# Loading the first weight chunk beside the first input tile, copies by PSUM bank and no GpSimd loads, in a two-layer feed-forward kernel

## Chip, cores, metric

One core of one Trainium2 chip. The metric is the device time of the core in microseconds (us), lower is better. A "run" is one execution; medians are over runs. "Head" is what happens from the start of the program until TensorE begins its steady stream of products.

## The reference, cut

```python
B, S, D, F = 1, 2048, 576, 4608          # all bfloat16
def reference(x, w1, b1, w2, b2):
    h = einsum("bsd,df->bsf", x, w1) + b1
    r = where(h > 0, h, 0)
    return einsum("bsf,fd->bsd", r * r, w2) + b2
```

## The kernel before

The rows of x are handled in four blocks of 512. For the first product x must lie transposed in SBUF (`xT`). For blocks 1 to 3 a DMA transposes it; block 0 is transposed by TensorE, 128 x 128 at a time. D = 576 is four chunks of 128 and one of 64. The first four column tiles of w1 (512 columns, `w1n`, chunks k = 0..3; `w1n8` is the 64-row rest) are loaded first and used while the remainder of w1 (`w1_h`, in column pieces and two 64-row halves) is coming.

The warm-up products and the first eight loads:

```python
wps = ps_o.tile([P, 512], FP32, name="wps", tag="po")
WARM = [512] * 6 + [128]
for i, n in enumerate(WARM):
    keep(nc.tensor.matmul(wps[:, 0:n], lhsT=ones[:, 0:P], rhs=ones[:, 0:n], start=True, stop=True))
# ...
load_x(nc.sync, 0)
load_x(nc.scalar, 1)
load_w1n(nc.sync, 0)
load_x(nc.scalar, 2)
load_w1n(nc.sync, 1)
load_x(nc.sync, 3)
for k in range(2, NK):
    load_w1n(nc.sync, k)
# ...
nc.gpsimd.dma_start(out=b1_rows[0:NFT, :], in_=b1.rearrange("(ft p) -> ft p", p=P))
nc.gpsimd.dma_start(out=b2_col[:], in_=b2[DM:D].rearrange("(d o) -> d o", o=1))
```

The head on TensorE. `x_transpose(j, k)` transposes chunk k of x tile j; `part(h, k)` is four products of 256 columns for half h of the block:

```python
for j in range(2):
    for k in range(NK):
        x_transpose(j, k)
for j in range(2):
    x_transpose(j, NK)
x_copies(0)            # PSUM to SBUF: chunks 0 to 3 have a bank each; VectorE and ScalarE by turns
part(0, 0)
for k in range(NK + 1):
    x_transpose(2, k)
part(0, 1)
part(0, 2)
for k in range(NK + 1):
    x_transpose(3, k)
x_copies(1)
dup_windows(0)
part(0, 3)
part(1, 0)
make_b1T()
for k in range(1, NK):
    part(1, k)
```

Then come pairs of 64-row products (`pair`, at the end of block 0's first four column tiles), and `a_rows`, which uses w1_h column by column: 18 products a column. Each load on a hardware queue waits, by the compiled program's semaphores, for the landing of the load eight places ahead of it, so at most eight are under way (in the changed kernel the ninth load is issued at 3.48 us, when the first of ScalarE's queue has landed at 3.47).

## Time and profile before

| | before |
|---|---|
| time, first three runs | 290.86 us median (290.51 to 291.31) |
| span of the profiled run | 289.6 us |
| x tile 0 landed; first transpose | 3.73; 3.77 us |
| first product of `part` | 4.87 us |
| TensorE at full clock from (clock record of the trace) | 6.51 us |
| first 64-row pair | 9.85 us |
| from there to the last product's end | 277.03 us |

The page of the kernel before: the span, busy time by engine, and the chain that ended last (each line there is an engine, a tile and a line of the kernel, with its share of the span).

```profile
span 289.6 us, 4693 instructions
...
PE 285.5 (99%) x2027; PEld 139.9 (48%) x2032; DVE 78.6 (27%) x176; ACT 96.7 (33%) x154; POOL 2.3 (1%) x10
...
PE 98%; DMA 1%; issue 0%; DVE 0%
```

TensorE is the bound, all the way. The only place with another limit is the head. The start of the chain of waits of before (start, duration, what; "x10" counts merged instructions; a piece begins where the one before it ends):

```profile
0.73 2.99 DMA x_sb<-in_x_dram
3.73 0.04 issue
3.77 1.25 PE tb L149 x10
5.02 0.86 PE pn L227 x4
5.88 0.53 PE tb L149 x5
6.42 0.98 PE pn L227 x8
7.40 0.28 PE tb L149 x5
7.68 0.87 PE pn L227 x8
```

Read the pace: four products in 0.86 us (215 ns each), later eight in 0.87 (109 ns each); five transposes in 0.53 us, later in 0.28. TensorE runs at half clock until about 6.5 us, and from 3.77 us on the chain is TensorE alone. No load after x tile 0 is on it.

### The profile page before, as it was taken

To read this page: it belongs to the slowest core of one execution; us is meant where nothing else is said; L and a number is where in the kernel's file an instruction comes from. 1 tells how busy PE (TensorE), PEld (TensorE's weight loads), DVE (VectorE), ACT (ScalarE), POOL (GpSimd) and SP (SyncE) were. 2 spreads that over 40 slices of the span, in tenths; PEclk is the share of its full clock that TensorE was granted. 3 is DMA by queue.
4 is the path that set the end of the run, shared out by engine and by line. 5 is a ranking of instruction groups with operands and counts; after the bars stand their busy time and mean duration, and the time that the engine had idled before them with its cause. 6 is when DMAs were issued, how large, how long until landed. Compare 5 with 4: busy or idle time off the path is not lost.

```text
span 289.6 us, 4693 instructions
## 1 busy us (share of the span) xinstructions
PE 285.5 (99%) x2027; PEld 139.9 (48%) x2032; DVE 78.6 (27%) x176; ACT 96.7 (33%) x154; POOL 2.3 (1%) x10
## 2 busy tenths in 40 slices
PE   8999999999999999999999999999999999999996
PEld 5544444444444555555544444444444455555555
DVE  1644554444500200000015444444440001100001
ACT  2566666666500000000027666666670000000000
POOL 3000000000000000000000000000000000000000
PEclk9999999999999999999999999999999999999999
DMA  7999999400001200000000000000000110000000
GB/s 198 221 245 188 308 389 212 92 0 2 0 14 25 52 16 18 16 16 18 16 16 2 1 2 0 2 0 2 0 2 0 36 38 16 16 16 19 33 16 18
DMA packets 31605, 16.52 MB, mean 57 GB/s; under 512 B 15700, under 2 KB 31584, under 8 KB 31584
## 3 DMA queue, kind: packets, MB, share of 16 engines
q1 hardware_dynamic: 31232, 15.91, 22.3%
q10 hardware_dynamic: 288, 0.30, 0.4%
q8 instruction: 16, 0.26, 0.4%
q14 instruction: 5, 0.04, 0.0%
q0 software_dynamic: 64, 0.01, 0.0%
HBM read 11.36 MB, written 2.36 MB: 47 GB/s over the span
## 4 chain that ended last, share of the span: by engine, by line
PE 98%; DMA 1%; issue 0%; DVE 0%
PE ph L188 42%; PE po L289 38%; PE pt L270 11%; PE pn L209 4%; PE pn L227 1%; DMA x_sb<-in_x_dram 1%; PE tb L149 1%; PE ph L190 1%; PE pn L203 1%; DVE o_sb L291 0%; PE b1T_ps L166 0%; PE pn L205 0%
## 5 line engine op out<-in xcount | busy, mean ns | idle before, releaser
L190 PE MATMUL ph<-xTw,w_h 64*128 64x512 bf16 x576 | 124.6, 376 | 0.0
L188 PE MATMUL ph<-xTw,w_h 64*128 64x512 bf16 x576 | 124.6, 376 | 0.0
L289 PE MATMUL po<-w_sb,hT 128*128 128x448 bf16 (+2 forms) x612 | 109.4, 341 | 0.0
L176 ACT ACTIVATE r<-ph,b1T 128x512 bf16<-128x512 f32 x128 | 81.1, 685 | 41.6 <-PE ph L190 41.6
L188 PEld LDWEIGHTS <-w_h 64*128 64x128 bf16 x576 | 54.1, 94 | 68.3
L289 PEld LDWEIGHTS <-hT 128*128 128x128 bf16 x612 | 58.5, 98 | 51.0
L177 DVE TENSOR_TENSOR hT<-r 128x512 bf16<-128x512 bf16 x144 | 61.2, 426 | 75.9 <-ACT r L176 75.5
L190 PEld LDWEIGHTS <-w_h 64*128 64x128 bf16 x576 | 54.1, 94 | 0.0
L291 DVE TENSOR_TENSOR o_sb<-po,b_bc 128x448 bf16<-128x448 f32 (+2 forms) x17 | 10.2, 597 | 125.8 <-PE po L289 125.8
L270 PE MATMUL pt<-hT,w_sb 128*128 128x512 bf16 x142 | 31.3, 379 | 0.1
L176 ACT ACTIVATE r<-pn,b1T 128x512 bf16<-128x512 f32 x16 | 10.3, 688 | 61.0 <-PE pn L205 59.6
L270 PEld LDWEIGHTS <-w_sb 128*128 128x128 bf16 x144 | 14.1, 98 | 17.0
L273 ACT ACTIVATE oT<-pt,b2T 128x512 bf16<-128x512 f32 x4 | 2.8, 688 | 28.3 <-PE pt L270 28.3
L209 PE MATMUL pn<-xTw,w1n 128*128 128x512 bf16 x45 | 10.4, 379 | 0.4 <-issue 0.3
L209 PEld LDWEIGHTS <-w1n 128*128 128x128 bf16 x48 | 4.5, 98 | 6.0 <-issue 0.8
L227 PE MATMUL pn<-xTw,w1n 128*128 128x256 bf16 x32 | 4.6, 295 | 0.0
L63 PE MATMUL wps<-const-bfloat16-1.0 128*128 128x512 bf16 (+1 forms) x7 | 2.8, 582 | 0.8 <-PEq L344 0.8
L227 PEld LDWEIGHTS <-w1n 128*128 128x128 bf16 x32 | 3.3, 107 | 0.5
L156 DVE COPY xTw<-tb 128x256 bf16<-128x256 bf16 x4 | 1.1, 292 | 6.7 <-PE tb L149 6.7
L119 DVE COPY xTw<-xTw 64x2048 bf16<-64x2048 bf16 x4 | 2.8, 690 | 0.2
L120 DVE COPY xTw<-xTw 64x2048 bf16<-64x2048 bf16 x4 | 2.7, 687 | 0.1
L149 PE MATMUL tb<-ident,x_sb 128*128 128x128 bf16 x20 | 2.4, 288 | 0.2 <-DMA x_sb<-in_x_dram 0.2
(23 smaller groups left out, 15.2 us busy)
## 6 DMA issues: line engine op xcount, KB each, us to landing
w_sb<-in_w_dram SPq DMA_DIRECT2D x4, 1296.0 KB, 12.7
w_h<-in_w_dram SPq DMA_DIRECT2D x14, 288.0 KB, 6.2
out_dram<-o_sb SPq DMA_DIRECT2D x15, 112.0 KB, 1.7
w_h<-in_w_dram SPq DMA_DIRECT2D x4, 144.0 KB, 3.5
w1n<-in_w_dram SPq DMA_DIRECT2D x4, 128.0 KB, 3.9
out_dram<-ot SPq DMA_DIRECT2D x4, 128.0 KB, 2.0
x_sb<-in_x_dram ACTq DMA_DIRECT2D x2, 144.0 KB, 2.9
x_sb<-in_x_dram SPq DMA_DIRECT2D x2, 144.0 KB, 3.4
```

The costliest lines, as they stand in the source:

```text
L63: keep(nc.tensor.matmul(wps[:, 0:n], lhsT=ones[:, 0:P], rhs=ones[:, 0:n], start=True, stop=True))
L149: keep(nc.tensor.transpose(bank[:, slot, qc], xs[:, j, c0:c0 + P], ident[:]))
L176: keep(nc.scalar.activation(out=r[:], in_=bank[:], func=ACT.Relu, bias=b1T[:, ft:ft + 1], scale=1.0))
L177: keep(nc.vector.tensor_tensor(out=hTs[sb][:, ft, :], in0=r[:], in1=r[:], op=ALU.mult))
L188: keep(nc.tensor.matmul(bx[:], lhsT=w1_h[0:H, LO_C[i], jc], rhs=xT[0:H, LO_W[i], :], start=(i == 0), stop=(i == NC - 1)))
L190: keep(nc.tensor.matmul(by[:], lhsT=w1_h[H:P, UP_C[i], jc], rhs=xT[H:P, UP_W[i], :], start=(i == 0), stop=(i == NC - 1)))
L203: keep(nc.tensor.matmul(banks[2 * i][:], lhsT=w1n8[0:H, i, :], rhs=xT[0:H, SPC, :], start=start, stop=stop, skip_group_check=order == "k_o ...
L209: keep(nc.tensor.matmul(banks[g][:], lhsT=w1n[:, k, g * P:(g + 1) * P], rhs=xT[:, O + k, :], start=start, stop=stop))
L227: keep(nc.tensor.matmul(banks[g][:, hc], lhsT=w1n[:, k, g * P:(g + 1) * P], rhs=xT[:, O + k, hc], start=(h == 0 and k == 0), stop=False, s ...
L270: keep(nc.tensor.matmul(pt[:], lhsT=w2_sb[:, ft, DM:D], rhs=hT[:, ft, :], start=(i == 0), stop=(i == NFT - 1)))
L289: keep(nc.tensor.matmul(po[:, 0:d1 - d0], lhsT=hT[:, ft, jj * P:(jj + 1) * P], rhs=w2_sb[:, ft, d0:d1], start=(i == 0), stop=(i == NFT - 1)))
L291: keep(nc.vector.tensor_tensor(out=o_sb[:, d0:d1], in0=po[:, 0:d1 - d0], in1=b2_bc[:, d0:d1], op=ALU.add))
```

## The change

The intent: have w1 chunk 0 as early as x tile 0, so that the first products can start; spread the other loads evenly over two queues; take the two small bias loads away from GpSimd; put several transposed chunks in one PSUM bank and copy bank by bank; fill the idle time ahead of x tile 0 by a longer last warm-up product (the warm-up products are called the filler below).

```diff
-    WARM = [512] * 6 + [128]
+    WARM = [512] * 6 + [256]
...
     load_x(nc.sync, 0)
-    load_x(nc.scalar, 1)
-    load_w1n(nc.sync, 0)
+    load_w1n(nc.scalar, 0, 1)
+    load_x(nc.sync, 1)
     load_x(nc.scalar, 2)
-    load_w1n(nc.sync, 1)
-    load_x(nc.sync, 3)
-    for k in range(2, NK):
-        load_w1n(nc.sync, k)
+    load_w1n(nc.sync, 1, 2)
+    load_x(nc.scalar, 3)
+    load_w1n(nc.sync, 2, 3)
+    load_w1n(nc.scalar, 3, 4)
...
-    nc.gpsimd.dma_start(out=b1_rows[0:NFT, :], ...)
-    nc.gpsimd.dma_start(out=b2_col[:], ...)
     keep(nc.scalar.activation(out=warm[:], ...))
+    keep(nc.scalar.dma_start(out=b1_rows[0:NFT, :], ...))   # b2_col: later, by SyncE
+    for h in range(2):
+        load_w1n8(nc.sync, h)          # all 512 columns to both halves; now ahead of w1_h
...
-    tb_po = [ps_o.tile([P, 2, HS], BF16, name="tb", tag="po") for _ in range(2)]
-    tb_ph = [ps_h.tile([P, 2, HS], BF16, name="tb", tag="ph") for _ in range(4)]
+    tb = [[ps_h.tile([P, 4, HS], BF16, name="tb", tag="ph") for _ in range(2)] for _ in range(2)]
+    PLACE = [(0, 0), (0, 1), (1, 0), (1, 1), (1, 2)]
...
+    def x_transpose(j):                # all five chunks of one tile; copies after the second tile
+        h, q = divmod(j, 2)
+        for bank, ks in enumerate((T_ORDER[:2], T_ORDER[2:])):
+            for k in ks:
+                ...transpose into tb[h][bank]
+            for k in ks if q == 1 else ():
+                copy = nc.scalar.copy if h == 1 and k in (2, 3) else nc.vector.tensor_copy
+                keep(copy(out=xT0[:, w, hc], in_=tb[h][bank][:, PLACE[k][1], :]))
...
                 for j in range(2):
-                    for k in range(NK):
-                        x_transpose(j, k)
...
+                    x_transpose(j)
+                for k in range(2):
+                    part(0, k)
+                    x_transpose(2 + k)
                 dup_windows(0)
+                for k in range(2, NK):
+                    part(0, k)
```

Also w2 is loaded in two pieces instead of four, and block 0's accumulators all lie in one pool.

More of the change, by code (lines that the diff above doesn't have):

```diff
@@ L57 @@
     ps_o = ctx.enter_context(tc.tile_pool(name="ps_o", bufs=4, space=PSUM))
-    wps = ps_o.tile([P, 512], FP32, name="wps", tag="po")
+    wps = ps_h.tile([P, 512], FP32, name="wps", tag="ph")
     ones = nc.const_aps.tensor(1.0, [P, 512], BF16)
-    WARM = [512] * 6 + [128]
+    WARM = [512] * 6 + [256]
     for i, n in enumerate(WARM):
@@ L66 @@
     w1n = wpool.tile([P, NK, GW], BF16, name="w1n")
-    w1n8 = wpool.tile([P, G // 2, P], BF16, name="w1n8")
+    w1n8 = wpool.tile([P, GW], BF16, name="w1n8")
     w1_h = wpool.tile([P, NC, FH], BF16, name="w1_h")
@@ L72, in load_x, with load_w1n @@
         keep(eng.dma_start(out=xs[:, rt, :], in_=x2[rt * P:(rt + 1) * P, :]))
-    def load_w1n(eng, k):
-        keep(eng.dma_start(out=w1n[:, k, :], in_=w1[k * P:(k + 1) * P, 0:GW]))
+    def load_w1n(eng, k0, k1):
+        src = w1[k0 * P:k1 * P, 0:GW].rearrange("(k p) f -> p k f", p=P)
+        keep(eng.dma_start(out=w1n[:, k0:k1, :], in_=src))
     def load_w1n8(eng, h):
-        src = w1[NK * P:D, 0:GW].rearrange("p (i h f) -> p i h f", h=2, f=P)
-        keep(eng.dma_start(out=w1n8[h * H:(h + 1) * H, :, :], in_=src[:, :, h, :]))
+        keep(eng.dma_start(out=w1n8[h * H:(h + 1) * H, :], in_=w1[NK * P:D, 0:GW]))
     def load_w1(eng, h, j0, j1):
@@ L83, in load_w1 @@
                       in_=w1_v[:, :, GW + h * FH + j0 * P:GW + h * FH + j1 * P]))
+    b1_rows = const.tile([P, P], BF16, name="b1_rows")
+    nc.vector.memset(b1_rows[:], 0.0)
     load_x(nc.sync, 0)
-    load_x(nc.scalar, 1)
-    load_w1n(nc.sync, 0)
+    load_w1n(nc.scalar, 0, 1)
+    load_x(nc.sync, 1)
     load_x(nc.scalar, 2)
-    load_w1n(nc.sync, 1)
-    load_x(nc.sync, 3)
-    for k in range(2, NK):
-        load_w1n(nc.sync, k)
+    load_w1n(nc.sync, 1, 2)
+    load_x(nc.scalar, 3)
+    load_w1n(nc.sync, 2, 3)
+    load_w1n(nc.scalar, 3, 4)
     ident = const.tile([P, P], BF16, name="ident")
     make_identity(nc, ident[:])
-    b1_rows = const.tile([P, P], BF16, name="b1_rows")
-    nc.gpsimd.memset(b1_rows[:], 0.0)
-    nc.gpsimd.dma_start(out=b1_rows[0:NFT, :], in_=b1.rearrange("(ft p) -> ft p", p=P))
-    b2_col = const.tile([P, 1], BF16, name="b2_col")
-    nc.gpsimd.dma_start(out=b2_col[:], in_=b2[DM:D].rearrange("(d o) -> d o", o=1))
-    b2T = const.tile([P, 1], FP32, name="b2T")
-    nc.gpsimd.tensor_copy(out=b2T[:], in_=b2_col[:])
     warm = const.tile([P, 1], FP32, name="warm")
     keep(nc.scalar.activation(out=warm[:], in_=nc.const_aps.tensor(0.0, [P, 1], FP32), func=ACT.Relu))
+    keep(nc.scalar.dma_start(out=b1_rows[0:NFT, :], in_=b1.rearrange("(ft p) -> ft p", p=P)))
+    for h in range(2):
+        load_w1n8(nc.sync, h)
     E3, O, SPC, E = 0, 1, 5, 6
@@ L130 @@
     w2_view = w2.rearrange("(ft p) d -> p ft d", p=P)
-    W2CH = 9
+    W2CH = 18
     def load_w2(c):
@@ L140 @@
     HS = SB // 2
-    tb_po = [ps_o.tile([P, 2, HS], BF16, name="tb", tag="po") for _ in range(2)]
-    tb_ph = [ps_h.tile([P, 2, HS], BF16, name="tb", tag="ph") for _ in range(4)]
-    half_banks = [tb_ph, None]
-    def x_transpose(j, k):
+    tb = [[ps_h.tile([P, 4, HS], BF16, name="tb", tag="ph") for _ in range(2)] for _ in range(2)]
+    PLACE = [(0, 0), (0, 1), (1, 0), (1, 1), (1, 2)]
+    T_ORDER = [0, 1, 2, 3, NK]
+    def x_transpose(j):
         h, q = divmod(j, 2)
-        qc = slice(q * P, (q + 1) * P)
-        bank, slot, c0 = (half_banks[h][k], 0, k * P) if k < NK else (half_banks[h][2], 1, D - P)
-        keep(nc.tensor.transpose(bank[:, slot, qc], xs[:, j, c0:c0 + P], ident[:]))
-    def x_copies(h):
         hc = slice(h * HS, (h + 1) * HS)
-        for k in range(NK):
-            src = half_banks[h][k][:, 0, :]
-            if k % 2 == 0:
-                keep(nc.vector.tensor_copy(out=xT0[:, O + k, hc], in_=src))
-            else:
-                keep(nc.scalar.copy(out=xT0[:, O + k, hc], in_=src))
-        keep(nc.vector.tensor_copy(out=xT0[:, E3, hc], in_=half_banks[h][2][:, 1, :]))
+        for bank, ks in enumerate((T_ORDER[:2], T_ORDER[2:])):
+            for k in ks:
+                slot = PLACE[k][1]
+                c0 = k * P if k < NK else D - P
+                keep(nc.tensor.transpose(tb[h][bank][:, slot, q * P:(q + 1) * P], xs[:, j, c0:c0 + P], ident[:]))
+            for k in ks if q == 1 else ():
+                w = O + k if k < NK else E3
+                copy = nc.scalar.copy if h == 1 and k in (2, 3) else nc.vector.tensor_copy
+                keep(copy(out=xT0[:, w, hc], in_=tb[h][bank][:, PLACE[k][1], :]))
     b1T = const.tile([P, NFT], FP32, name="b1T")
     def make_b1T():
-        b1T_ps = ps_o.tile([P, P], BF16, name="b1T_ps", tag="po")
+        b1T_ps = ps_h.tile([P, P], BF16, name="b1T_ps", tag="ph")
         keep(nc.tensor.transpose(b1T_ps[:], b1_rows[:], ident[:]))
@@ L198, in a_full @@
         for g in range(G):
-            pool, tag = (ps_o, "po") if g < 2 else (ps_h, "ph")
+            pool, tag = (ps_o, "po") if g < 2 or order == "k_outer" else (ps_h, "ph")
             banks.append(pool.tile([P, SB], FP32, name="pn", tag=tag))
         def pair(i, start, stop):
-            keep(nc.tensor.matmul(banks[2 * i][:], lhsT=w1n8[0:H, i, :], rhs=xT[0:H, SPC, :],
+            keep(nc.tensor.matmul(banks[2 * i][:], lhsT=w1n8[0:H, 2 * i * P:(2 * i + 1) * P], rhs=xT[0:H, SPC, :],
                              start=start, stop=stop, skip_group_check=order == "k_outer"))
-            keep(nc.tensor.matmul(banks[2 * i + 1][:], lhsT=w1n8[H:P, i, :], rhs=xT[H:P, E3, :],
+            keep(nc.tensor.matmul(banks[2 * i + 1][:], lhsT=w1n8[H:P, (2 * i + 1) * P:(2 * i + 2) * P], rhs=xT[H:P, E3, :],
                              start=start, stop=stop, skip_group_check=order == "k_outer"))
@@ L220, in a_full @@
             if order == "k_outer":
-                tb_new = [ps_h.tile([P, 2, HS], BF16, name="tb", tag="ph") for _ in range(2)]
-                half_banks[1] = tb_new + tb_po
                 def part(h, k):
@@ L231, in a_full @@
                 for j in range(2):
-                    for k in range(NK):
-                        x_transpose(j, k)
-                for j in range(2):
-                    x_transpose(j, NK)
-                x_copies(0)
-                part(0, 0)
-                for k in range(NK + 1):
-                    x_transpose(2, k)
-                part(0, 1)
-                part(0, 2)
-                for k in range(NK + 1):
-                    x_transpose(3, k)
-                x_copies(1)
+                    x_transpose(j)
+                for k in range(2):
+                    part(0, k)
+                    x_transpose(2 + k)
                 dup_windows(0)
-                part(0, 3)
+                for k in range(2, NK):
+                    part(0, k)
                 part(1, 0)
@@ L296 @@
         load_w1(nc.sync, 1, j0, j1)
-        if j0 == 0:
-            load_w1n8(nc.sync, 0)
-            load_w1n8(nc.sync, 1)
     load_xT(1)
@@ L303 @@
         load_w1(nc.sync, 1, j0, j1)
+    b2_col = const.tile([P, 1], BF16, name="b2_col")
+    keep(nc.sync.dma_start(out=b2_col[:], in_=b2[DM:D].rearrange("(d o) -> d o", o=1)))
+    b2T = const.tile([P, 1], FP32, name="b2T")
+    nc.gpsimd.tensor_copy(out=b2T[:], in_=b2_col[:])
     keep(nc.sync.dma_start(out=b2_bc[:], in_=b2.partition_broadcast(P)))
-    for c in (0, 2, 1, 3):
+    for c in range(2):
         load_w2(c)
```

## The prediction

> **What bounds the kernel.** The page's first part has TensorE busy 285.5 of 289.6 us; the chain of waits is 98% TensorE. From the first L203 pair (9.85 us) to the last product (286.9 us) the matmul timeline has no gap over 0.16 us, and is left alone. Only the head can move.
>
> **The head of before** (matmul timeline, single instructions):
> - Seven warm-up matmuls from 0.78; then 0.17 us idle until x tile 0 lands at 3.73.
> - From 3.77 TensorE has practically no idle: 20 transposes, the b1 transpose, 32 products of 256 columns. No load is late: w1 chunks landed at 4.32, 5.86, 6.47, 7.05, used at 4.87, 6.21, 6.69, 7.51.
> - The clock record reaches full speed only at 6.51. Before it a transpose takes 107 ns and a 256-column product 213 ns; after it 56 and 109. At full speed all 53 need 21 x 0.056 + 32 x 0.109 = 4.7 us; 2.74 us at half clock cost 1.37 us more: 3.77 + 4.7 + 1.37 = 9.8, as seen.
>
> The Trainium skill ("TensorE: Matmul & The Clock Gate", Part 1) says the array runs at half rate until a busy window of a free-running 3.4 us counter has passed, so the moment varies between runs. The trace agrees: full speed 5.74 us after the first matmul.
>
> **What the change does.**
> - x0 still goes first on SyncE beside one load of like size: landing at 3.6 to 3.75. x1 becomes second on SyncE (issued at 1.2; the load in that place landed at 4.32). It is needed after five x0 transposes, at 3.77 + 5 x 0.107 = 4.30: just in time, perhaps 0.1 us late.
> - First copy: VectorE copies take 0.29 us. The first product starts at about 4.95 instead of 4.87.
> - No GpSimd loads: those packets ran from 3.65 to 5.3 us, while the DMA rate fell from 350 to 170-215 GB/s. Without them later loads should land 0.5 to 1 us earlier, but TensorE didn't wait for them.
> - The b1 load moves behind the ACT table load (1.28 us): issued at about 4.3, landed at about 7, needed at 8.3.
> - w1n8 grows by 64 KB and moves ahead of w1_h. w1_h columns 2 to 4 landed at 13.16, used at about 14.2: still in time.
> - Banks, w2 in two loads, b2 by SyncE: off the path. 128 more warm-up columns (0.107 us) fill idle time.
>
> On the critical path: -0.1 (x0, filler) + 0.1 (x1, first copy) - 0.1 (smaller waits, clock) = about -0.1 us. The clock's phase is larger: a switch 1 us earlier or later should (estimate) move the end by 0.5 us, which fits the spread of before, 290.51 to 291.31.
>
> **Predicted: 290.7 us, 8 in 10 between 290.1 and 291.3.** Faster by over 2%: 1%; within 2%: 98%; slower by over 2%: 1%.
>
> **What would show it.** Right: x0 lands within 0.2 us of 3.7; first 256-column product at 4.8 to 5.0; first 64-row pair at 9.2 to 10.2, following the start of full clock by half; no DMA dip at 4.2 to 5.2 us; 277 us from the first pair to the last product. Wrong: idle TensorE before the x1 or b1 transposes; a wait for w1_h at its second or third column.
>
> **What would make it wrong.** Full clock coming systematically earlier: up to 1 us faster. x1 or b1 late: up to 0.5 us slower.

## More of the kernel before

One trap. The windows view has a column for the granted clock, the last but two (the columns are the window, its length, busy time of PE, PEld, DVE, ACT and POOL, clock, DMA share, GB/s). For the kernel before:

```profile
0.80:3.60 2.80, 2.80 (x7) 0.84 (x7) 0.00 (x0) 1.49 (x2) 1.80 (x5) 1.00 0.63 184
4.20:5.10 0.90, 0.90 (x10) 0.82 (x9) 0.33 (x2) 0.47 (x2) 0.00 (x0) 1.00 0.87 197
```

It says 1.00 where the products run at half pace, because the first clock record comes only at the switch to full speed. In a head, trust the pace of equal products, not this column.

## The result, and the profile after

| | before | after |
|---|---|---|
| time, six runs each | 290.92 us (290.51 to 291.52) | 291.15 us (290.95 to 291.52) |
| span of the profiled run | 289.6 | 289.2 |
| x0 landed; first transpose | 3.73; 3.77 | 3.66; 3.70 |
| first product of `part` | 4.87 | 5.11 |
| full clock from | 6.51 | 4.51 |
| first 64-row pair | 9.85 | 9.49 |
| from there to the last product's end | 277.03 | 277.03 |

The ratio of the changed kernel to before is 1.0008 with a 95% interval of 0.9994 to 1.0022: the same within noise. A ratio is the mean time of one kernel's fast runs over that of the other's fast runs of the same rounds, so it is not quite the ratio of the medians quoted.

The page of the changed kernel, the same lines:

```profile
span 289.2 us, 4697 instructions
...
PE 285.5 (99%) x2032; PEld 139.1 (48%) x2032; DVE 79.0 (27%) x179; ACT 96.1 (33%) x152; POOL 0.9 (0%) x7
...
PE 99%; DVE 0%; issue 0%
```

And the chain of waits of its head:

```profile
0.77 2.93 PE wps L63 x7
3.71 0.71 PE tb L150 x5
4.42 0.00 issue
4.42 0.33 PE tb L150 x2
4.74 0.02 issue
4.77 0.30 DVE xTw L154
5.07 0.04 issue
5.11 0.60 PE pn L218 x4
5.71 0.28 PE tb L150 x5
5.99 0.44 PE pn L218 x4
6.42 0.28 PE tb L150 x5
```

Full clock came 2 us earlier here than in the profile of before (four products take 0.44 us at 5.99), which by itself should take 1 us from the head. The head was only 0.36 us shorter. The difference went into waits that before did not have: the transposes of x1 start at 4.42, though those of x0 were done issuing at 3.70 + 5 x 0.107 = 4.24; and a VectorE copy stands on the chain, for which TensorE waits from 4.74 to 5.11.

So the first question was whether the change had brought the early clock. The second was where the rest went.

### The profile page after: what moved, and what is told of

It is laid out like the page before. It is cut to its first block, busy times and chain, and to the rows that moved or that the text cites. A ratio compares the mean times of both kernels' runs of the same rounds, so it can differ in the third digit from the quotient of the medians.

```text
span 289.2 us, 4697 instructions
## 1 busy us (share of the span) xinstructions
PE 285.5 (99%) x2032; PEld 139.1 (48%) x2032; DVE 79.0 (27%) x179; ACT 96.1 (33%) x152; POOL 0.9 (0%) x7
## 4 chain that ended last, share of the span: by engine, by line
PE 99%; DVE 0%; issue 0%
PE ph L182 42%; PE po L272 38%; PE pt L253 11%; PE pn L203 4%; PE pn L218 1%; PE wps L63 1%; PE ph L184 1%; PE pn L197 1%; PE tb L150 1%; DVE xTw L154 0%; DVE o_sb L274 0%; PE b1T_ps L160 0%; PE pn L199 0%
## 5 line engine op out<-in xcount | busy, mean ns | idle before, releaser
L218 PE MATMUL pn<-xTw,w1n 128*128 128x256 bf16 x32 | 4.0, 273 | 0.2 <-DVE xTw L154 0.2
L154 DVE COPY xTw<-tb 128x256 bf16<-128x256 bf16 x8 | 1.9, 284 | 4.9 <-PE tb L150 4.6
L197 PE MATMUL pn<-xTw,w1n 64*128 64x512 bf16 x8 | 2.4, 379 | 0.0
```

The lines of the kernel that those rows point to most:

```text
L197: keep(nc.tensor.matmul(banks[2 * i][:], lhsT=w1n8[0:H, 2 * i * P:(2 * i + 1) * P], rhs=xT[0:H, SPC, :], start=start, stop=stop, skip_grou ...
L218: keep(nc.tensor.matmul(banks[g][:, hc], lhsT=w1n[:, k, g * P:(g + 1) * P], rhs=xT[:, O + k, hc], start=(h == 0 and k == 0), stop=False, s ...
```

## The experiments

**The sum used below.** All 21 transposes and 32 products of the head take about 4.7 us at full clock (21 x 0.056 + 32 x 0.109). So

*first 64-row pair = first transpose + 4.7 + half of the time from there to full clock + waits.*

For before: 3.77 + 4.7 + 1.37 = 9.84 against 9.85 measured, waits 0. For after: 3.70 + 4.7 + 0.40 = 8.80 against 9.49, waits 0.69 us.

Two theories. A: the moment of full clock is chance; a late clock hides late loads, an early one lays them bare, and the change made the loads and copies that matter later. B: the change itself (its longer filler) brought the early clock.

### Both kernels again: e1, e2, e10

No edit; each gives a second or third profile, and five runs.

> The kernel before, unchanged, for a second profile and for its spread. Theory A (the moment of full clock is a matter of chance, and the head is limited by the clock when it comes late and by the loads when it comes early): the full-clock record starts anywhere between 4.2 and 7.6 us, and the first 64-row pair starts between 9.5 us (clock at 4.5) and 9.9 us (clock at 6.5). Theory B (the change itself brought the full clock 2 us earlier, by its longer filler): the record starts at 6.4 to 6.6 us again and the pair at 9.85. Time 290.5 to 291.5 either way, ratio 1.000.

> The changed kernel, unchanged, for a second profile. Theory A: full clock at another moment than 4.51 us; if it comes at 6.5, the first 64-row pair starts near 10.1 us, 0.25 us later than in the kernel before at that clock. Theory B: full clock at 4.5 again, pair at 9.5. Time 290.9 to 291.5, ratio to before 1.000 to 1.002.

> The changed kernel a third time. Theory A: same sum plus what it waits for: 0.2 to 0.3 us before x1's transposes and 0.2 us before the first product at a clock early enough, about 0.3 us in all at a late one. First 64-row pair 9.1 to 10.2 us, median 290.9 to 291.3, over the repaired kernel's median of this batch by 0 to 0.5 us.

| | full clock | first transpose | first pair | waits in head | last product's end |
|---|---|---|---|---|---|
| before | 6.51 | 3.77 | 9.85 | 0.0 | 286.88 |
| e1, before | 6.21 | 3.73 | 9.68 | 0.0 | 286.71 |
| after | 4.51 | 3.70 | 9.49 | 0.7 | 286.52 |
| e2, after | 3.46 | 3.48 | 9.09 | 0.9 | 286.55 |
| e10, after | 3.42 | 3.69 | 9.26 | 0.9 | 286.95 |

Medians: e1 290.92 (ratio 0.9992, 0.9979 to 1.0006), e2 291.13 (1.0007, 0.9995 to 1.0020), e10 291.20 (1.0011, 0.9999 to 1.0023).

In e2 and e10 the clock came a whole 3 us before that of the first profile of before, and still the last product ends at about the same time. Part of the gain was lost in the head: x1 landed at 4.18 in e2 by the chain, while x0's transposes, at full clock, were done issuing at 3.48 + 5 x 0.056 = 3.76. The TensorE timeline of e2 has the transposes of x0 and then those of x1 (start, time until the last of the group ends, and the idle time ahead in brackets):

```profile
3.48 0.44 PE L150 MATMUL tb<-ident,x_sb 128*128 128x128 bf16 x5
4.22 0.45 PE L150 MATMUL tb<-ident,x_sb 128*128 128x128 bf16 x5 [0.30 <-DMA x_sb<-in_x_dram]
```

Another part was lost after it, in a wait that neither first profile has. The list of waits in e2, weight loads of TensorE, from 9 to 30 us:

```profile
PEld L184 <- DMA w_h<-in_w_dram: 0.5, 1, 0.5
```

And the chain of waits of e10 from 9 us on:

```profile
8.86 5.33 DMA w_h<-in_w_dram
14.20 0.05 issue
14.24 0.39 PE ph L184
```

That is the upper half of w1_h columns 2 and 3. It landed at 13.79 in e2 and 14.20 in e10, and TensorE had come that far at about 13.4 and 13.6: waits of 0.42 and 0.66 us, which is why the pair-to-end distance there is 277.45 and 277.69 instead of 277.03. In the first profile of before this load landed at 13.16 and was used at 14.18. The margin is thin in both kernels once the clock is early: in five profiles of before's body it landed at 13.01 to 13.71, and e7 (below), with an early clock, had it at 13.30 and needed it at about 13.5.

Theory B in its plain form fails here: the two kernels' TensorE streams are the same until 128 columns into the last warm-up product, which starts at 3.28 us, so until about 3.39. The clock switched at 3.46 and 3.42; by then a longer filler had added at most 0.07 us of work.

The clock records say more. In the thirteen profiles that have one, full clock lasted either 283.31 or 286.72 us. These differ by 3.41 us and are 83 and 84 times that: the clock changes on a grid of 3.41 us steps only. One step ahead of the switch lies at 3.10 us in before, 2.79 in e1 and 2.45 in e5 (before's filler too, below), when both kernels' fillers were still the same; so the shorter filler did not make these clocks late. e6 (below), with the longer filler, did not switch at the step at 3.33, 2.55 us after its first product, and e10 did at 3.42, 2.65 us after. Where the steps lie against the start of the program differs from execution to execution, and that is the chance in theory A.

But the expectation of e1 "anywhere between 4.2 and 7.6" was too late by 0.8 us: full clock can come within 2.7 us of the first product.

### One part alone: the filler, e7

```diff
-    WARM = [512] * 6 + [128]
+    WARM = [512] * 6 + [256]        # e7, on the kernel before
```

> The kernel before with only the last warm-up matmul lengthened from 128 to 256 columns. Theory B (filler fills the gap and brings the clock early): full clock at 3.4 to 4.6 us, as in the three profiles with the changed kernel's body. Theory A (free-running): anywhere from 3.4 to 6.8; if it comes at about 4.5, the first 64-row pair starts near 9.55 us, because w1 chunk 1 and chunk 2 are then waited for (0.3 and 0.15 us), not 1 us earlier than before. Time 290.5 to 291.3.

Measured: 290.90 (ratio 0.9994, 0.9981 to 1.0008). This trace has no clock record; the spacing of the transposes changes from 107 to 56 ns at 4.4 us. That gives a profile of before's body at an early clock, to set beside after's at 4.51. The start of its chain of waits:

```profile
0.78 2.93 PE wps L63 x7
3.71 1.00 PE tb L149 x10
4.71 0.04 issue
4.75 0.60 PE pn L227 x4
```

The ten transposes go through without a break and the first product starts 1.09 us after the first transpose (1.41 in the changed kernel at nearly the same clock). First pair at 9.20 against 9.49, waits 0.47 us against 0.69, last product's end at 286.23 against 286.52. My figure of 9.55 was too high, as w1 chunk 1 landed at 5.57 here, not at 5.86. So at an early clock the changed kernel is 0.29 us behind; the later start and clock of its profile explain 0.07 of that, which leaves 0.22 for the change, in this one pair of profiles.

### One part alone: no GpSimd loads, e5

```diff
-    nc.gpsimd.dma_start(out=b1_rows[0:NFT, :], ...)     # on the kernel before
-    nc.gpsimd.dma_start(out=b2_col[:], ...)
+    keep(nc.scalar.dma_start(out=b1_rows[0:NFT, :], ...))   # after ScalarE's warm-up
+    keep(nc.sync.dma_start(out=b2_col[:], ...))             # after w1_h
```

> The kernel before, with one part of the change alone: no loads by GpSimd (b1 rows by ScalarE after its warm-up, b2 late on SyncE). If the GpSimd loads slowed the others, the DMA dip at 4.2 to 5.1 us (170 to 215 GB/s) is gone (250 or more) and x tile 3 and w1 chunk 3 land 0.3 to 0.8 us before 6.07 and 7.05. As TensorE waited for neither at a late clock, the time stays within 0.3 us of before, ratio 0.999 to 1.001. Rival: the dip comes from the second and later loads themselves, and stays. Start of the full clock, if free-running: anything from 3.4 to 6.8 us; if it belongs to the kernel before: 5.9 to 6.5 again; if GpSimd loads were what delayed it: 3.4 to 4.5.

Measured: 291.00 (ratio 0.9997, 0.9983 to 1.0010), full clock at 5.87, first pair at 9.37 = 3.46 + 4.7 + 1.2, waits 0. The windows view of the stretch from 4.2 to 5.1 us, which in before has 197 GB/s. The changed kernel:

```profile
4.20:5.10 0.90, 0.69 (x8) 0.36 (x6) 0.33 (x2) 0.00 (x0) 0.00 (x0) 1.00 1.03 326
```

e5:

```profile
4.20:5.10 0.90, 0.90 (x8) 0.75 (x7) 0.65 (x3) 0.65 (x2) 0.00 (x0) 1.00 0.93 291
```

With GpSimd loads the four profiles have 197, 252, 246 and 256 GB/s there (before, e1, e7, e11); without them 291 (e5), and 326, 349 and 319 in the changed kernel. So the dip goes with those loads, though 256 and 291 are not far apart against its scatter. But the loads that matter hardly landed sooner. x tile 3 landed at 6.07, 5.88, 5.75 and 5.67 with GpSimd loads, at 5.78 (e5) and 5.49, 5.88 and 6.15 (changed kernel) without; the last of the first eight at 7.05, 6.66, 6.55 and 6.31 with, at 6.67 and 6.66, 6.57 and 6.83 without. What the dip cost is less than the scatter between executions. One thing spoils e5 as a clean test of the last of these: its b1 load is now one of the first eight on the hardware queues, so w1 chunk 3 is the ninth and was issued at 3.61 instead of 3.12.

### Undoing one part: x tile 1 first, e6

```diff
     load_x(nc.sync, 0)
-    load_w1n(nc.scalar, 0, 1)      # on the changed kernel
-    load_x(nc.sync, 1)
+    load_x(nc.scalar, 1)
+    load_w1n(nc.sync, 0, 1)
```

> The changed kernel with x tile 1 put back as first load on ScalarE and w1 chunk 0 second on SyncE. If the late x1 is the loss: no TensorE idle between the x0 and x1 transposes (0.2 to 0.3 us in the two profiles of the changed kernel), and the first product starts 0.95 us after the first transpose at full clock, 1.27 us at half clock (1.41 us in both profiles of the changed kernel, 1.10 in those of before). The rest of that distance is the copy that waits for both tiles of its bank. Time 0.1 to 0.3 us under the changed kernel's 291.1 where the clock is alike: 290.7 to 291.1.

Measured: 291.04 (290.36 to 291.47, ratio 0.9995, 0.9980 to 1.0011). x1 landed at 3.77. The ten transposes of x0 and x1 are one group in the TensorE timeline:

```profile
3.65 1.25 PE L150 MATMUL tb<-ident,x_sb 128*128 128x128 bf16 x10
```

There is no break between them, and the first product comes 1.31 us after the first transpose at half clock. The clock came at 6.74, the latest of all profiles with a filler, and the first pair at 10.01 = 3.65 + 4.7 + 1.55 + 0.11 of waits. The wait for x1 is gone; the time of the profiled run, 291.47, tells nothing, as its clock is not that of the other profiles. Nor do the times show the gain by themselves: the ratio is below the changed kernel's 1.0008, but the intervals overlap.

### The structure without the loads: e3 and e4

Both kernels got the same first eight loads in the same order, with x tile 0 the last, 16 warm-up products of 512 columns, and no GpSimd loads. This was meant as a gate: nothing of the head should start until all loads are there and the clock is full.

```diff
-    WARM = [512] * 6 + [128]           # e3, on before; e4, on after, the same from its own lines
+    WARM = [512] * 16
-    (its first eight loads)
+    load_x(nc.sync, 1);     load_w1n(nc.scalar, 0)
+    load_w1n(nc.sync, 1);   load_x(nc.scalar, 2)
+    load_w1n(nc.sync, 2);   load_x(nc.scalar, 3)
+    load_w1n(nc.scalar, 3)
+    load_x(nc.sync, 0)
```

> The kernel before with the loads of both bias vectors taken from GpSimd, x tile 0 made the last of the first eight loads, and 16 warm-up matmuls of 512 columns: every load has landed and the clock is full before the first transpose, so only the structure of the head (order of transposes, banks, copies) is left. Estimate: x0 lands near 6.7 us, TensorE's filler ends between 5.9 and 7.6, the head needs 4.7 us at full clock and up to 0.3 us of waits for copies, first 64-row pair at 11.7 to 12.5 us, time 292.8 to 293.8. Theory A: the spread of the runs shrinks where the filler always ends before x0 lands, to about 0.4 us from 1.0. Rival (spread comes from the DMAs or the launch): spread stays at 1 us.

> The changed kernel under the same gate: same first eight loads in the same order, same 16 warm-up matmuls. If the new order of transposes and the copies on one engine are harmless by themselves (all of the loss is x1 arriving late), it is within 0.1 us of the gated kernel before, and the gap before its first 256-column product is like that one's. If the structure costs time, it is 0.1 to 0.3 us longer, with idle TensorE before the first product. Time 292.8 to 294.0.

Measured: e3 293.62 (292.86 to 293.96), e4 293.15 (292.40 to 293.57). As a test of the spread this was inconclusive: the runs spread by 1.1 and 1.2 us, because the gate did not hold. The filler's own length depends on the clock (full clock at 5.88 in e3, 3.44 in e4), and the same eight loads landed up to 0.9 us apart in the two executions. (What was issued behind them is not the same, from 3.64 us pieces of w1_h of 144 KB in e3, from 3.71 pieces of w1n8 of 64 KB in e4, which may be part of that.) As a look at the structure it works, since both heads ran at full clock. The TensorE timeline of e3:

```profile
6.74 0.72 PE L145 MATMUL tb<-ident,x_sb 128*128 128x128 bf16 x10
7.56 0.60 PE L223 MATMUL pn<-xTw,w1n 128*128 128x256 bf16 x4
```

and of e4:

```profile
5.80 0.73 PE L150 MATMUL tb<-ident,x_sb 128*128 128x128 bf16 x10
6.75 0.60 PE L218 MATMUL pn<-xTw,w1n 128*128 128x256 bf16 x4 [0.21 <-DVE xTw L154]
```

First transpose to first product: 0.82 in e3, 0.95 in e4; to the first pair 5.02 and 5.15. So in this one pair of profiles the tile-by-tile order with a copy that waits for both chunks of its bank costs about 0.12 us, apart from any load.

### Is it the clock? No filler, e11

```diff
-    WARM = [512] * 6 + [128]           # on the kernel before
+    WARM = []
```

> The kernel before without any warm-up matmul: TensorE starts at x0's landing, 3.7 us. Theory A: full clock 2.7 to 6.1 us after the first transpose, so at 6.4 to 9.8 us instead of 3.4 to 6.8; first 64-row pair 9.8 to 11.5 us; median 291.6 to 293.0 (estimate 292.2), so the clock's moment shows in the time at half its delay (3 us later, 1.3 us slower). If the clock were not what limits the head, the time stays at 290.9.

Measured: 291.95 (291.20 to 292.11), ratio 1.0032 (1.0020 to 1.0044): 1.0 us slower than before, near the estimate. Two pieces of its chain of waits:

```profile
6.20 1.71 PE pn L227 x8
...
8.38 0.87 PE pn L227 x8
```

Eight products that took 0.98 us in before take 1.71 here. Full clock came at 8.17 us, and the sum gives 3.56 + 4.7 + 2.31 = 10.57 for the first pair; it was 10.55. In the profiles without load waits the half-rate sum holds for moments of the clock from 4.46 (e8, below) to 8.17, a range of 3.7 us.

### Three repairs together: e8 and e9

```diff
     load_x(nc.sync, 0)                                       # on the changed kernel
+    load_x(nc.scalar, 1)
+    load_w1n(nc.sync, 0, 1)                                  # as in e6
...
+    load_w1(nc.scalar, 1, 0, 1)        # upper halves of w1_h columns 0 and 1, after b1_rows
+    load_w1(nc.scalar, 1, 1, 2)
...
+    def x_transpose(js):               # x_transpose((0, 1)): both tiles of bank 0, then of bank 1
+        for bank, ks in enumerate((T_ORDER[:2], T_ORDER[2:])):
+            for j in js:
+                ...transposes of ks
+            ...copies of this bank
```

> The changed kernel with three repairs: x tile 1 first on ScalarE; both tiles' transposes of one bank before those of the next, so that the first copies run under the remaining six transposes; and the upper halves of w1_h columns 0 and 1 issued by ScalarE, since SyncE's issues of 0.68 us each set the pace there. Expected: first product 0.7 to 0.9 us after the first transpose at full clock, 1.1 at half clock; the second half of w1_h columns 2 and 3 lands at 11.8 to 12.9 us instead of 12.93 to 13.79, so no wait for it at any clock; first 64-row pair 9.0 to 9.3 us at an early clock, 9.7 to 9.9 at a late one; time 290.4 to 290.9, ratio 0.998 to 1.000. If neither load order nor copies matter because the clock decides all, 290.9 to 291.2 again.

> The repaired kernel unchanged, for more times and a second moment of the clock. If the clock's moment decides (theory A): whatever it is, the first 64-row pair starts at x0's first transpose + 4.75 us + half of the time from that transpose to full clock, within 0.15 us, because no load or copy is waited for; 8.6 to 9.9 us. Median 290.5 to 291.2, spread over 1 us. If the repairs are worth a steady 0.5 us, the median is at or below 290.5.

In the two profiles the repairs do what they should. The chain of waits of e8:

```profile
0.77 2.93 PE wps L63 x7
3.70 1.00 PE tb L153 x10
4.71 0.45 PE pn L221 x4
5.15 0.28 PE tb L153 x5
5.43 0.44 PE pn L221 x4
5.87 0.28 PE tb L153 x5
6.15 1.31 PE pn L221 x12
```

Nothing but TensorE, with no wait for a copy or a load. With the clock at 4.46 (e9: 4.77) the first pair starts at 8.76 (8.88), waits 0.05 (0.03), and w1_h's third and fourth columns land at 12.64 (12.77), so nothing is given back: the last product ends at 285.79 (285.93) against 286.23 to 286.95 in the other profiles with an early clock (e7, after, e2, e10).

The times do not follow. e8: 290.37, 291.68, 291.82, 291.30, 290.39, 290.40 (ratio 0.9998, 0.9978 to 1.0017). e9: 290.50, 291.99, 290.56, 291.60, 292.08, 292.55 (ratio 1.0021, 1.0001 to 1.0042). Five runs lie at 290.4 to 290.6 and seven at 291.3 to 292.6; both profiled runs are of the first sort. e8's median, 290.85, lies where it was expected, e9's, 291.79, does not. A late clock, at the 6.74 seen in e6, would by the sum add 1.1 us to e8. The slowest run is 2.2 us slower than the fastest, so something else happens in them that no profile caught. Its four fastest runs beat every run of before (290.51 at best), but it is not a faster kernel: its median over both groups is 291.45 against about 290.9.

### x tile 0 in two halves: e12

```diff
-    load_x(nc.sync, 0)                  # on the repaired kernel; x0's rows 0-63 and 64-127
-    load_x(nc.scalar, 1)
-    load_w1n(nc.sync, 0, 1)
+    load_xh(nc.sync, 0, 0)
+    load_xh(nc.scalar, 0, 1)
+    load_x(nc.sync, 1)
+    load_w1n(nc.scalar, 0, 1)           # then x2, w1 k1, x3, w1 k2, w1 k3
-    WARM = [512] * 6 + [256]
+    WARM = [512] * 5 + [384]
```

> The repaired kernel with x tile 0 loaded in two halves of 64 rows, one on each queue, ahead of everything, and the filler cut to end at 3.2 us. x0 has 72 KB a queue ahead of it instead of 144: it should land at 3.1 to 3.3 us instead of 3.4 to 3.7. As the work from there runs at half clock until full clock comes (its moment does not move), 0.35 us earlier gives about 0.2 us. First 64-row pair 8.5 to 9.7 us, median 290.3 to 291.0. Rival: the first landing is bound by latency, not by bytes: x0 lands at 3.4 or later, and w1 chunk 3, pushed back by one issue, may be waited for.

Measured: 291.96 (291.34 to 292.97), ratio 1.0040 (1.0025 to 1.0055): a miss. The halves landed at 2.98 and 3.40, the second where the rival in the expectation had put it, so TensorE began at 3.44 and won 0.1 us; w1 chunk 0 came only at 5.00 (TensorE idle 0.52 us before the first product) and x2 at 6.00 (0.39). Full clock came at 3.91 and the first pair at 10.07 = 3.44 + 4.7 + 0.24 + 1.69 of waits. So this edit cost far more than the half-size first load won. What in it did so stays open: it puts one more load ahead of the others, but it also takes x1 back to SyncE and w1 chunk 0 to ScalarE, as in the changed kernel, and w1 chunk 3 to SyncE.

## Why the prediction was right or wrong

The time (290.7 forecast, 290.1 to 291.3; 291.15 measured) and "within 2%" were right, and so was the main reading: only the head can move, TensorE is its limit, and the moment of full clock outweighs all parts of the change. The sum with half of the cold time predicts the first pair within 0.05 us in all five profiles without load waits (before, e1, e5, e8, e9), and in e11.

That the time lay in the range is no proof of the small terms: the range is 1.2 us wide, and before itself, at 290.92, lies in it as well.

The net of the small terms had the wrong sign. I forecast -0.1 us. Measured was about +0.2: the ratios of the three sessions are 1.0008, 1.0007 and 1.0011, and over all runs the changed kernel's mean is 291.22 (16 runs) against 290.98 for before (42 runs with e1). Each session's interval includes 1; the three together point to a loss of 0.08%. That the waits below make up this loss is read from profiles; no timing run separates it. The terms:

- **"x1 ... just in time, perhaps 0.1 us late", "the first product starts at about 4.95 instead of 4.87."** Mis-sized. In three profiles the first product came 1.41, 1.41 and 1.33 us after the first transpose instead of my 1.18, and 1.1 in before's body. x1 was late by 0.2 us at a half clock and by 0.4 to 0.5 at a full one, because an earlier clock also brings forward the moment at which it is needed. I had costed x1 only for the clock of the one profile I had. e6 shows the load order as the cause of that wait, e3 and e4 put 0.12 us on the order of transposes and copies. By the sum the head waited 0.7 to 0.9 us in all, where the +0.1 was forecast.
- **"-0.1 (smaller waits, clock)."** There were no waits to make smaller: by the sum the head of before has none in either profile.
- **"No GpSimd loads ... later loads should land 0.5 to 1 us earlier."** Wrong. The DMA dip went, as foretold, but the landings stayed where they were within their scatter (e5). That TensorE wouldn't gain from it was right.
- **"w1_h columns 2 to 4 ... still in time."** True in the first profile of the changed kernel, false in e2 and e10, where it cost 0.42 and 0.66 us. There an early clock reached this load before it landed: a gain in the head was given back 4 us later. I had listed this as a sign of being wrong.
- **"-0.1 (x0, filler)."** x0 landed at 3.66, 3.40 and 3.64, against 3.73 and 3.68: a small gain within the scatter. The filler by itself (e7) shows no difference in time.
- **The clock.** "Full clock coming systematically earlier" was named as the risk. Theory B in the form "the filler does it" is refuted by e2 and e10, where the clock came with next to none of the added work done, and by the grid of before, e1 and e5. With a filler in place full clock came at 3.42, 3.44, 3.46, 3.9, 4.4, 4.46, 4.51, 4.77, 5.87, 5.88, 6.21, 6.51 and 6.74, early and late ones for both bodies and their variants. Still, the three profiles with the 128-column end of the filler (before, e1, e5) were all late, and of the seven with 256 columns only e6 was. That is few; a tendency for some other reason, such as where in the grid a program starts, is not excluded.

What the Trainium skill says ("TensorE: Matmul & The Clock Gate", Part 1: a free-running window of 3413 ns, so the number of cold products changes from run to run) agrees with these traces: with a filler the moments lie between 3.42 and 6.74 us, a range of 3.32 us, and the records of full clock last whole multiples of 3.41 us. Its main text ("Trainium Kernel Development and Optimization", Key Constraints) also says that loads from several queues run on the same 16 engines and interleave, and that using several queues saves only issue time. That fits in part: the last of the first eight loads landed at 6.57 to 6.83 us in the changed kernel with four loads a queue, at 6.31 to 7.05 in before's body with six and two; moving w1 chunk 0 forward only moved x1 back. But the order of the loads matters in a way that nothing here explains: with x1 and w1 chunk 0 exchanged, still four a queue (e6, e8, e9), the last of the eight landed at 6.01, 5.91 and 6.18, 0.4 to 0.9 us earlier.

Open: what makes seven of the twelve runs of the repaired kernel 1 to 2 us slower than the other five; whether the kernel after really meets an early clock more often; why the order of e6 brings in the first eight loads sooner; and why the same loads land at different times in executions of the same program.

## What to carry to other kernels

In a head where TensorE is still at half clock, draw up the sum: first start + work at full clock + half of the cold time + waits. A single profile of such a kernel shows one moment of the clock only; take several before costing a load as "in time", because a late clock hides late loads and an early one uncovers them. Give the first slots of the queues to the tiles needed first by TensorE's own order (here both x tiles of the first half, not the weights), and see to it that what an earlier head will reach next is there too.

## What the Trainium skill lacked or had wrong

- "TensorE: Matmul & The Clock Gate", Part 1, gives about 3.4 us of sustained work before full clock. Here it came 2.65 to 2.69 us after the first product in three profiles (e10, e4, e2: first product at 0.77, full clock at 3.42, 3.44 and 3.46), which suggests that a partly idle window suffices; 2.55 us, in e6, did not.
- The same page, Part 4, says that full clock does not engage for transposes. In these traces the transposes were issued each 107 ns before the switch and each 56 ns after it. Whether transposes alone would bring the switch, no run shows.
- Beyond the sharing of the 16 engines, no page that I read says what small loads by GpSimd cost the others while they run: 197 to 256 GB/s at 4.2 to 5.1 us with them (four profiles), 287 to 384 without (ten, in several load orders), though in e5, without them, no landing moved beyond its scatter.
- No page that I read gives the scatter of landings between executions of the same program: the last of the first eight loads landed at 7.05 and 6.66 us in two profiles of before, and x tile 0 at 3.66, 3.40 and 3.64 in three of the changed kernel.
